# Attention with a mixture of adapters: value products on halves of the array, in two runs for each pair of heads

## The chip, the cores and the metric

The kernel runs on one core of one Trainium2 chip. The metric is the device time of one execution in microseconds. Before the change three runs gave a median of 231.32 us (231.14 to 232.71). Lower is better.

## What is computed

The reference has two parts. The first is attention with a relative position bias for 8 batches of 8 heads, 576 positions and 64 values a head:

```python
scores = q @ k.T / 8 + bias[bucket(|i - j|)]      # one bias table per head, 32 buckets
attn   = exp(scores - max) / sum(exp(scores - max))
x      = attn @ v                                 # heads side by side: 4608 rows of 512
```

All distances of 128 and more share one bucket, so the bias differs from a constant only in a band around the diagonal. The second part works on each row of x:

```python
logits = x @ w_gate                    # 8 experts; the best two are kept
w      = softmax over those two
out    = x + sum_e w[e] * (x @ A[e]) @ B[e]       # A: 512 x 16, B: 16 x 512
```

## The kernel before

**Units.** A unit is one batch and one pair of heads (a pair of heads fills the 128 partitions with its 2 x 64 values); there are 32 units in order, four to a batch. Scores are made transposed: keys on partitions, queries along the free axis. The keys of a head are four chunks of 128 (j = 0 to 3) and a tail of 64; the tails of a pair's two heads share one tile of 128 partitions (pe), while the chunks are in pm, laid out head, chunk, query.

**Slots.** The 4 x 576 = 2304 columns of a pair's chunks are cut into slots of 512, so a unit has six slots: s = 0 to 3 with 512 columns a head, s = 4 with the last 256, s = 5 for the tails. In each slot TensorE (PE) makes the scores of two heads on rows 0 to 63 and 64 to 127 of the array (lines 256 and 266) into one of two PSUM buffers, and ScalarE (ACT) takes the exponential of the slot in one instruction (lines 260 and 268). The scores of a slot therefore wait for the exponential of two slots earlier.

**The order is written by hand.** The loop at the end of the kernel names, for each slot, what every engine gets next; each engine works through its own list in that order. p is the unit before u; its products with the values are made during u. In a unit from the second batch on:

- slot 0: scores; on VectorE (DVE) the bias of chunk 3 of p; on PE the value products of chunk 0 of p, then the eight transposes of the next unit's keys and queries (line 224);
- slot 1: scores; an adapter step; DVE: bias of p's tail (line 274); value products of chunk 1; DVE copies the transposed keys and queries out (line 228);
- slot 2: scores, value products of chunk 2; slot 3: scores, an adapter step, value products of chunk 3, DVE: bias of chunk 0 of u;
- slot 4: scores, value products of p's tail; once a batch the transposes of the next batch's tails and their copy;
- slot 5: scores, an adapter step; DVE: finish p (reciprocal, line 313, and the normalising product, line 314), then bias of chunks 1 and 2 of u (line 285).

The bias is a product of the exponentials with a table of exponentials.

**Value products.** `values(u, j)` makes ten matmuls: five tiles of 128 queries for each head. For a chunk both operands have 128 keys on 128 partitions; for the tail, 64 keys, and the two heads lie on the two halves of the array. All of a pair accumulate in one PSUM tile of two banks (pv, a pool with one buffer), one bank a head, with 65 columns a query tile: 64 values and a column of ones that gives the sum. The first value product of a pair thus waits for line 314 of the pair before.

**Adapter steps.** When a batch is finished, its rows are put in groups of three tiles of 128, and each group becomes a queue of steps, each with a part for PE and one for DVE: transposes of x (line 342), logits and A (line 355, copied out by ACT, then the gates on DVE and GpSimd), transposes of the weighted z (line 394), and one product with B a tile (line 403), added to x on DVE (line 407) and stored. `place(slot)` emits the DVE part of the step before and puts the PE part of the next one into the given slot, after that slot's scores; `place(None)` emits the PE part at once. PE parts use a PSUM pool with two buffers (mm), which the transposes of keys, queries and tails use too.

**Last pairs.** In the first and the last unit of the last batch `early` packs the value products of p into slots 1 to 3 and finishes p in slot 3. After the loop, the products of the last pair alternate with the transposes of the last five tiles (class Last); these go through the mm pool, the third lot through the pool of the scores.

**Loads.** SyncE (SP) issues the loads of a batch head by head, two batches ahead; GpSimd (POOL) casts them to bf16, one pair at a time.

Of the kernel before, what the change touches and what calls it, by code (L numbers as in the profile page):

```python
# [11 lines left out]
FP32 = mybir.dt.float32  # L12
# [21 lines left out]
def kernel(  # L34
# [11 lines left out]
    nc = tc.nc  # L46
    B, H, S, D = q.shape
# [5 lines left out]
    HP = H // 2  # L53
# [6 lines left out]
    W = D + 1  # L60
# [81 lines left out]
    pool_cast = nc.gpsimd.tensor_copy  # L142
# [69 lines left out]
    xs, xe, probs, accs = {}, {}, {}, {}  # L212
    tps = {}

    def batch_tiles(b):
        if b not in qkT:
            qkT[b] = ldp.tile([128, HP, 2, S], BF16, name="qkT", tag="qkT")
        return qkT[b]

    def transpose_pe(u):  # L220
        ps = tps[u] = mp.tile([128, 2, 4, 128], BF16, name="tp", tag="mm")
        for i in range(2):
            for j in range(4):
# [46 lines left out]
    def bias(u, j, n=1):  # L270
        b, hp = units[u]
        pm, pe = probs[u]
        if j == 4:
            nc.vector.tensor_tensor(pe[:, S - TE:], pe[:, S - TE:],
                                    _ap(ebe, hp * TE + TE - 1, [[-1, TE]]), op=ALU.mult)
            return
        q0, q1 = max(0, (j - 1) * 128), min(S, (j + 2) * 128)
        e0 = 2 * hp * TW + TW - 1 - (q0 - (j - 1) * 128)
        w = q1 - q0
        if n == 1:  # L280
            t, e = pm[:, :, j * S + q0:j * S + q1], _ap(eb, e0, [[TW, 2], [-1, w]])
        else:
            t = _ap(pm, j * S + q0, [[4 * S, 2], [S + 128, n], [1, w]])
            e = _ap(eb, e0, [[TW, 2], [0, n], [-1, w]])
        nc.vector.tensor_tensor(t, t, e, op=ALU.mult)  # L285

    def values(u, j):
        b, hp = units[u]
        pm, pe = probs[u]
        vm, ve = vals[b % 2]  # L290
        if j == 0:
            accs[u] = pvp.tile([128, 2, 512], FP32, name="pv", tag="pv")
        pv = accs[u]
        for t in range(5):
            tok = min(t * 128, S - 128)
            for h in range(2):
                if j < 4:
                    lhsT = pm[:, h, j * S + tok:j * S + tok + 128]
                    rhs = vm[:, j, 2 * hp + h, :W]
                else:  # L300
                    keys = slice(h * 64, (h + 1) * 64)
                    lhsT, rhs = pe[keys, tok:tok + 128], ve[keys, hp, :W]
                nc.tensor.matmul(pv[:, h, t * W:(t + 1) * W], lhsT=lhsT, rhs=rhs,  # L303
                                 start=(j == 0 and t == 0), stop=(j == 4),
                                 skip_group_check=True)

    def normalise(u):
        b, hp = units[u]
        pv = accs.pop(u)
        if hp == 0:  # L310
            xs[b] = xp.tile([128, 5, Dm], BF16, name="xn", tag="xn")
        rc = ms.tile([128, 2, 5], FP32, name="rc", tag="rc")
        nc.vector.reciprocal(rc, _ap(pv, D, [[512, 2], [W, 5]]))  # L313
        nc.vector.tensor_tensor(  # L314
            _ap(xs[b], hp * 128, [[D, 2], [Dm, 5], [1, D]]),
            _ap(pv, 0, [[512, 2], [W, 5], [1, D]]),
            _ap(rc, 0, [[5, 2], [1, 5], [0, D]]), op=ALU.mult)
# [131 lines left out]
    def at(slot, fn, *args):  # L449
        due.setdefault(slot, []).append((fn, args))  # L450

    def place(pe_slot):
        if state["now"]:
            state["now"]()
            state["now"] = None
        if queue:
            pe, dve = queue.popleft()
            state["now"] = dve or (lambda: None)
            if pe is None:
                pass  # L460
            elif pe_slot is None:
                pe()
            else:
                at(pe_slot, pe)
# [114 lines left out]
    NU = len(units)  # L579

    def finish(p, t):
        normalise(p)
        if units[p][1] == HP - 1:
            at(t + 1, batch_done, units[p][0])

    for t in range(SLOTS * NU):
        u, s = divmod(t, SLOTS)
        b, hp = units[u]
        p = u - 1
        scores(u, s)  # L590
        for fn, args in due.pop(t, []):
            fn(*args)
        if u == 3:
            load_adapters(s)
        for i in range(3 if u < 2 else 2 if s % 3 == 0 else 1):
            if loading:
                loading.popleft()()
        early = u >= NU - HP and hp in (0, HP - 1)
        if s == 0:
            if u == 0:  # L600
                while loading:
                    loading.popleft()()
                loading = load(1)
            if p >= 0:
                bias(p, 3)
                if not early:
                    values(p, 0)
            if HP <= u < NU - 1:
                transpose_pe(u + 1)
            place(t + 1)  # L610
        if s == 1:
            if p >= 0:
                bias(p, 4)
                values(p, 1)
            if u + 1 < NU:
                if u >= HP:
                    transpose_out(u + 1)
                cast_v(u + 1, pool_cast)
        if s == 2:
            if p >= 0:  # L620
                values(p, 2)
                if early:
                    values(p, 3)
            if u + 2 < NU:
                cast_qk(u + 2, 0, pool_cast)
            place(t + 1)
        if s == 3:
            if p >= 0:
                values(p, 4 if early else 3)
            bias(u, 0)  # L630
            if early:
                finish(p, t)
        if s == 4:
            if p >= 0 and not early:
                values(p, 4)
# [12 lines left out]
        if s == 5:  # L648
            if u < HP:
                transpose_out(u + 1)  # L650
            if p >= 0 and not early:
                finish(p, t)
            if hp == 2 and b + 1 < B:
                cast_tails(b + 1, pool_cast)
            bias(u, 1, 2)
            if u in (NU - HP - 1, NU - 2, NU - 1):
                values(u, 0)
            if b >= B - 2:
                place(t + 1)


    u = NU - 1
    bias(u, 3)
    while state["now"] or queue:
# [2 lines left out]
                fn(*args)  # L667
        place(0)
    last = Last(B - 1)
    join(B - 1, 0, 384)  # L670
    values(u, 1)
    last.head_pe(0, 2, mp, "mm")
    bias(u, 4)
    values(u, 2)
    last.head_pe(2, 2, mp, "mm")
    values(u, 3)
    last.head_pe(4, 1, scp, "sc")
    values(u, 4)
    normalise(u)
    join(B - 1, 384, Dm)  # L680
    last.zl_pe(0, 3)
# [31 lines left out]
```

## Time and profile before

| | us |
|---|---|
| median of three runs | 231.32 |
| the profiled execution, its own time | 233.92 |
| its span, first to last instruction | 231.8 |
| exponentials, lines 260 and 268, ACT busy | 142.2 + 20.8 |
| value products of the chunks, line 303, PE busy | 63.0 |
| value products of the tails, line 303, PE busy | 10.2 |
| bias products of the chunks, line 285, DVE busy | 67.6 |
| normalising product, line 314, DVE busy | 26.4 |

The profile page gives, for each engine, the time in which it worked and the share of the span; then a chain, followed back from the last instruction, at each step to what released it. The waits say, for each instruction that an engine stood idle before, who ended that: total us, times, longest. A row of the timeline has a start, a duration, the engine, the line, the operation, out<-in, the shape (for a matmul first rows*columns of the array) and the count, and in brackets how long the engine had been idle and what ended that. PE overlaps matmuls, so the time from one start to the next says more of its pace than a duration. A row of the windows has a stretch, its length, busy us (and instructions) of PE, PE's weight loads, DVE, ACT and POOL, then the share of its clock that PE was granted, the DMA share and GB/s.

### The profile page before, as it was taken

How to read it: one execution, taken by the hardware profiler on the slowest of the kernel's cores; microseconds unless marked ns; L12 is line 12 of the kernel's file. 1: busy time of each engine (PE TensorE's matmuls, PEld its weight loads, DVE VectorE, ACT ScalarE, POOL GpSimd, SP SyncE). 2: the span in 40 equal slices, each digit the busy share in tenths (PEclk: the TensorE clock that was granted, in tenths of full speed). 3: DMA queues.
4: the chain of work that ended last, by engine and by line, in shares of the span. 5: the costliest groups of instructions: out<-in, count | busy, mean ns of one | idle time of the engine just before them, and what ended most of it. 6: DMA issues, size and time to landing. Idle time of an engine off the chain costs nothing.

```text
span 231.8 us, 7224 instructions
## 1 busy us (share of the span) xinstructions
PE 181.6 (78%) x2900; PEld 121.7 (52%) x2900; DVE 174.9 (75%) x401; ACT 174.0 (75%) x225; POOL 97.1 (42%) x171
## 2 busy tenths in 40 slices
PE   0797857989899976888899976897888887796661
PEld 0354534666566663564566664565565655464530
DVE  5346763878798869787998869987988788987760
ACT  3587954999899876879789876897988767877422
POOL 2316497249413613805903613916507443411010
PEclk9999985999999999899999999999999999999955
DMA  7899899878879998797597785976597122222206
GB/s 163 199 244 221 188 161 208 186 165 202 196 170 234 223 247 203 208 246 184 137 229 185 210 201 146 251 172 173 114 230 214 48 77 73 90 48 95 90 29 199
DMA packets 126521, 39.74 MB, mean 171 GB/s; under 512 B 120464, under 2 KB 121880, under 8 KB 126488
## 3 DMA queue, kind: packets, MB, share of 16 engines
q1 hardware_dynamic: 120056, 38.62, 68.2%
q0 software_dynamic: 4832, 0.27, 3.5%
q10 hardware_dynamic: 1600, 0.40, 0.8%
q8 instruction: 22, 0.36, 0.6%
q14 instruction: 11, 0.09, 0.1%
HBM read 29.84 MB, written 9.45 MB: 169 GB/s over the span
## 4 chain that ended last, share of the span: by engine, by line
DVE 36%; PE 34%; ACT 8%; SPq 8%; issue 6%; DMA 4%; POOL 2%; POOLq 0%; ACTq 0%
DVE pm L285 12%; PE pv L303 11%; PE sc L256 9%; DVE xn L314 7%; ACT pm L260 7%; DVE ot L407 6%; SPq L101 5%; PE dl L403 2%; PE xT_ps L342 2%; DVE xT L347 2%; DVE rc L313 2%; PE tp L224 2%; PE zl L355 2%; DMA q<-in_q_dram 2%; DVE qkT L237 1%
## 5 line engine op out<-in xcount | busy, mean ns | idle before, releaser
L260 ACT ACTIVATE pm<-sc 128x1024 bf16<-128x1024 f32 (+1 forms) x160 | 142.2, 939 | 31.2 <-PE sc L256 30.2
L303 PE MATMUL pv<-vm,pm 128*128 128x65 bf16 x1280 | 63.0, 197 | 9.2 <-DVE xn L314 9.1
L285 DVE TENSOR_TENSOR pm<-pm,eb 128x512 bf16<-128x512 bf16 (+2 forms) x96 | 67.6, 725 | 2.4 <-DMA eb<-gx_d 1.9
L303 PEld LDWEIGHTS <-pm 128*128 128x128 bf16 x1280 | 51.2, 99 | 33.8 <-issue 20.7
L256 PE MATMUL sc<-qkT 64*128 64x384 bf16 (+7 forms) x512 | 61.9, 300 | 4.7 <-ACT pm L260 1.8
L370 POOL TENSOR_TENSOR ls<-z,top 128x24 f32<-128x24 f32 (+1 forms) x11 | 4.1, 372 | 66.1 <-DVE top L368 57.5
L256 PEld LDWEIGHTS <-qkT 64*128 64x128 bf16 x512 | 19.2, 95 | 20.8 <-issue 6.6
L224 PE MATMUL tp<-ident,qkn 128*128 128x128 bf16 x256 | 21.1, 227 | 10.5 <-DVE qkn L129 5.6
L228 DVE COPY qkT<-tp 128x1024 bf16<-128x1024 bf16 x32 | 21.9, 683 | 8.9 <-PE tp L224 8.9
L314 DVE TENSOR_TENSOR xn<-pv,rc 128x640 bf16<-128x640 f32 x32 | 26.4, 824 | 1.1
L133 POOL CAST vm<-v 128x512 bf16<-128x512 f32 x32 | 22.1, 690 | 10.3 <-DMA v<-in_v_dram 10.3
L129 POOL CAST qkn<-q 128x512 bf16<-128x512 f32 x30 | 23.1, 771 | 3.0 <-DMA q<-in_q_dram 1.5
L129 POOL CAST qkn<-k 128x512 bf16<-128x512 f32 x32 | 20.9, 652 | 6.6 <-DMA k<-in_k_dram 6.5
L268 ACT ACTIVATE pe<-sc 128x576 bf16<-128x576 f32 x32 | 20.8, 650 | 3.2 <-PE sc L266 2.2
L224 PEld LDWEIGHTS <-qkn 128*128 128x128 bf16 x256 | 15.9, 101 | 11.8 <-DVE qkn L129 5.6
L407 DVE TENSOR_TENSOR ot<-dl,xn 128x512 f32<-128x512 f32 x28 | 19.1, 683 | 2.8 <-PE dl L403 2.8
L266 PE MATMUL sc<-qkT 64*64 64x64 bf16 (+1 forms) x128 | 14.1, 294 | 7.5 <-ACT pm L260 7.3
L403 PE MATMUL dl<-Bc,zT 128*128 128x512 bf16 x31 | 12.2, 393 | 4.3 <-DVE ot L407 3.7
L313 DVE RECIPROCAL rc<-pv 128x10 f32<-128x10 f32 x32 | 6.9, 215 | 10.2 <-PE pv L303 10.2
L347 DVE COPY xT<-xT_ps 128x1024 bf16<-128x1024 bf16 (+1 forms) x20 | 11.2, 562 | 1.2 <-PE xT_ps L342 1.2
L266 PEld LDWEIGHTS <-qkT 64*64 64x64 bf16 x128 | 6.7, 105 | 9.3 <-issue 6.8
L385 POOL TENSOR_TENSOR gate<-nu,rd 128x24 f32<-128x24 f32 (+1 forms) x11 | 2.6, 239 | 19.4 <-DVE rd L383 8.7
(87 smaller groups left out, 164.8 us busy)
## 6 DMA issues: line engine op xcount, KB each, us to landing
q<-in_q_dram SPq DMA_DIRECT2D x64, 128.0 KB, 3.1
v<-in_v_dram SPq DMA_DIRECT2D x64, 128.0 KB, 2.9
k<-in_k_dram SPq DMA_DIRECT2D x62, 128.0 KB, 2.9
out_dram<-ot SPq DMA_DIRECT2D x28, 256.0 KB, 2.2
qke<-in_q_dram SPq DMA_DIRECT2D x8, 128.0 KB, 2.8
ve<-in_v_dram SPq DMA_DIRECT2D x16, 64.0 KB, 2.6
out_dram<-otL SPq DMA_DIRECT2D x4, 256.0 KB, 2.0
qke<-in_k_dram SPq DMA_DIRECT2D x7, 128.0 KB, 2.8
```

Of the source, the lines that this page charges most:

```text
L129: eng(out=nats[u][:, i].rearrange("p j (h d) -> p j h d", h=2), in_=src)
L133: eng(out=vals[b % 2][0][:, :, 2 * hp:2 * hp + 2, :D], in_=staged[b][2][:, :, 2 * hp:2 * hp + 2, :])
L224: nc.tensor.transpose(ps[:, i, j, :], nats[u][:, i, j, :], ident)
L228: nc.vector.tensor_copy(batch_tiles(b)[:, hp, :, :512], tps.pop(u).rearrange("p i j t -> p i (j t)"))
L256: nc.tensor.matmul(sc[:, h, c - SW * s:c - SW * s + w], lhsT=kT[rows, j * 128:(j + 1) * 128], rhs=qT[rows, q0:q0 + w], start=True, stop=True)
L260: nc.scalar.activation(pm[:, :, SW * s:end], sc[:, :, :n], ACT.Exp, scale=scale)
L266: nc.tensor.matmul(flat[rows, q0:q0 + n], lhsT=kT[rows, 512:], rhs=qT[rows, q0:q0 + n], start=True, stop=True)
L268: nc.scalar.activation(pe, flat[:, :S], ACT.Exp, scale=scale)
L285: nc.vector.tensor_tensor(t, t, e, op=ALU.mult)
L303: nc.tensor.matmul(pv[:, h, t * W:(t + 1) * W], lhsT=lhsT, rhs=rhs, start=(j == 0 and t == 0), stop=(j == 4), skip_group_check=True)
L314: nc.vector.tensor_tensor(_ap(xs[b], hp * 128, [[D, 2], [Dm, 5], [1, D]]), _ap(pv, 0, [[512, 2], [W, 5], [1, D]]), _ap(rc, 0, [[5, 2], [1, ...
L407: nc.vector.tensor_tensor(ot, self.dl, self.x[t], op=ALU.add)
```

## The change

`values` takes a run, cross = 0 or 1, and the chunks to be made. Each product has 64 keys: the two halves of the array work on different heads at once. In run 0 the lower half takes head 0 and the upper half head 1, in run 1 the other way round, so that in both the halves write to different banks. The tails, which lie on halves already, belong to run 0. A pair has 50 products in run 0 and 40 in run 1.

Run 0 of p is made as a block in slot 1, run 1 in slot 4. The bias of p's tail moves to slot 0, behind that of chunk 3. The transposes of the next unit move from slot 0 to slot 2, the copy of their result from slot 1 to slot 3 (in the first four units they stay in slots 4 and 5). Of the three adapter steps of a unit the one of slot 1 is now emitted in slot 0, right behind the scores; in the last two batches the fourth step, which stood in slot 0, follows run 0 in slot 1. The `early` cases go. After the loop the last pair's run 0 is finished first, then come the transposes of the last tiles, all in the mm pool, then run 1.

```diff
-    def values(u, j):
+    def values(u, cross, *js):
         b, hp = units[u]
         pm, pe = probs[u]
         vm, ve = vals[b % 2]
...
+        for j in js:
+            if j == 0 and not cross:
+                accs[u] = pvp.tile([128, 2, 512], FP32, name="pv", tag="pv")
+            pv = accs[u]
+            for t in range(5):
+                tok = min(t * 128, S - 128)
+                for half in range(2):
+                    h = half ^ cross
+                    keys = slice(half * 64, (half + 1) * 64)
+                    if j < 4:
+                        lhsT = pm[keys, h, j * S + tok:j * S + tok + 128]
+                        rhs = vm[keys, j, 2 * hp + h, :W]
+                    else:
+                        lhsT, rhs = pe[keys, tok:tok + 128], ve[keys, hp, :W]
+                    nc.tensor.matmul(pv[:, h, t * W:(t + 1) * W], lhsT=lhsT, rhs=rhs,
+                                     start=(j == 0 and t == 0 and not cross),
+                                     stop=(j == 3 and cross == 1),
+                                     skip_group_check=True)
...
         if s == 0:
...
             if p >= 0:
                 bias(p, 3)
-                if not early:
-                    values(p, 0)
+                bias(p, 4)
+            place(None)
+        if s == 1:
+            if p >= 0:
+                values(p, 0, 0, 1, 2, 3, 4)
+            if u + 1 < NU:
+                cast_v(u + 1, pool_cast)
+            if b >= B - 2:
+                place(None)
+        if s == 2:
             if HP <= u < NU - 1:
                 transpose_pe(u + 1)
-            place(t + 1)
...
             place(t + 1)
         if s == 3:
+            if HP <= u < NU - 1:
+                transpose_out(u + 1)
+            bias(u, 0)
+        if s == 4:
             if p >= 0:
-                values(p, 4 if early else 3)
...
+                values(p, 1, 0, 1, 2, 3)
...
         if s == 5:
...
-            if p >= 0 and not early:
+            if p >= 0:
                 finish(p, t)
...
-            if u in (NU - HP - 1, NU - 2, NU - 1):
-                values(u, 0)
-            if b >= B - 2:
-                place(t + 1)
+            if u == NU - 1:
+                values(u, 0, 0, 1, 2)
...
     last = Last(B - 1)
+    bias(u, 4)
+    values(u, 0, 3, 4)
+    last.head_pe(0, 2, mp, "mm")
     join(B - 1, 0, 384)
-    values(u, 1)
-    last.head_pe(0, 2, mp, "mm")
-    bias(u, 4)
-    values(u, 2)
     last.head_pe(2, 2, mp, "mm")
-    values(u, 3)
-    last.head_pe(4, 1, scp, "sc")
-    values(u, 4)
+    last.head_pe(4, 1, mp, "mm")
+    values(u, 1, 0, 1, 2, 3)
     normalise(u)
```

More of the change, by code (lines that the diff above doesn't have):

```diff
@@ L290, in values @@
         vm, ve = vals[b % 2]
[L291 to L305, printed above, removed]
+        for j in js:
[16 more added lines that the diff above has]
+                                     skip_group_check=True)
     def normalise(u):
@@ L597 @@
                 loading.popleft()()
-        early = u >= NU - HP and hp in (0, HP - 1)
         if s == 0:
@@ L605 @@
                 bias(p, 3)
-                if not early:
-                    values(p, 0)
+                bias(p, 4)
[8 more added lines that the diff above has]
+        if s == 2:
             if HP <= u < NU - 1:
                 transpose_pe(u + 1)
-            place(t + 1)
[L611 to L623, printed above, removed]
             if u + 2 < NU:
@@ L627 @@
         if s == 3:
+            if HP <= u < NU - 1:
+                transpose_out(u + 1)
+            bias(u, 0)
+        if s == 4:
             if p >= 0:
-                values(p, 4 if early else 3)
[L630 to L633, printed above, removed]
-            if p >= 0 and not early:
-                values(p, 4)
+                values(p, 1, 0, 1, 2, 3)
             if u + 2 < NU:
@@ L650 @@
                 transpose_out(u + 1)
-            if p >= 0 and not early:
+            if p >= 0:
                 finish(p, t)
```

## The prediction

> **What bounds the kernel now.** I read the page's busy shares and chain first.
>
> ```profile
> PE 181.6 (78%) x2900; PEld 121.7 (52%) x2900; DVE 174.9 (75%) x401; ACT 174.0 (75%) x225; POOL 97.1 (42%) x171
> DVE 36%; PE 34%; ACT 8%; SPq 8%; issue 6%; DMA 4%; POOL 2%; POOLq 0%; ACTq 0%
> ```
>
> Three engines are busy for three quarters of the span, none for all of it, and the chain hops between DVE and PE. So the pace is set by a loop between these two. The waits name its links:
>
> ```profile
> ACT pm L260 <- PE sc L256: 30.2, 49, 4.2
> DVE rc L313 <- PE pv L303: 10.2, 14, 2.2
> PE pv L303 <- DVE xn L314: 9.1, 14, 1.2
> ```
>
> ACT starves for scores (30.2 us). DVE's reciprocal waits for the last value product (only 14 of 32 times: otherwise DVE itself is late), and the next pair's first value product waits for DVE to empty the one accumulator. I call the start of a pair's reciprocal R. The timeline's reciprocals stand at 114.52 (unit 16) and 165.14 (unit 24): 6.33 us from R to R. ACT's exponentials alone need 5.0.
>
> What a value product costs shows in the timeline of PE:
>
> ```profile
> 105.75 0.48 PE L303 MATMUL pv<-vm,pm 128*128 128x65 bf16 x10
> 106.16 0.39 PE L256 MATMUL sc<-qkT 64*128 64x192 bf16 x4
> 106.48 0.39 PE L403 MATMUL dl<-Bc,zT 128*128 128x512 bf16 x1
> 106.71 0.47 PE L303 MATMUL pv<-vm,pm 128*128 128x65 bf16 x10
> 107.12 0.28 PE L256 MATMUL sc<-qkT 64*128 64x256 bf16 x2
> 107.24 0.31 PE L303 MATMUL pv<-ve,pe 64*128 64x65 bf16 x10
> 107.48 0.40 PE L234 MATMUL tpe<-ident,qke 128*128 128x128 bf16 x4
> ```
>
> Read starts. 256 score columns followed by 64-row products take 0.12 us (107.12 to 107.24), 512 followed by a 128-row product 0.32 (106.16 to 106.48), not 0.24: leaving one row mode for the other costs 0.08 to 0.1. Ten 128-row products and such an exit take 0.41, so 0.031 each. Ten 64-row ones and an exit take 0.24 (107.24 to 107.48): 0.14 for five couples, 0.028 a couple.
>
> **The change, part by part.**
>
> *PE's work.* Before, a pair has 40 products on 128 rows and 10 on 64; after, 90 on 64 rows, 45 couples. 32 pairs: 1280 x 0.031 + 160 x 0.028 = 44.2 us against 1440 x 0.03 = 43.2 (I take 0.03). Mode changes, counted in the two instruction orders, fall from 314 to 222: 92 x 0.1 = 9.2 us. So PE gives up 10 us in all, 0.32 a pair.
>
> A rule speaks against this. The Trainium skill, "TensorE: Matmul & The Clock Gate", section "LDWEIGHTS (loading the stationary operand)", says that a weight load's time goes by its columns, so half the rows cost as much; an estimate from its figure (128 columns at 1.2 a ns, 107 ns a load) makes the 1280 loads more 137 us if they stood in a row. In the trace ten 64-row loads take 0.30 us, ten 128-row ones 0.36, so two halves load together. I go by the rows.
>
> *The loop.* Before, each chunk of keys has its own slot, and the late bias products are needed late: chunk 3's by slot 3, the tail's by slot 4. After, the first run holds chunks 0 to 3 and the tail in one block in slot 1; its last four products need the tail's bias, and the scores of slot 2 stand behind them on PE. DVE's order up to there:
>
> ```profile
> 152.47 0.22 DVE L313 RECIPROCAL rc<-pv 128x10 f32<-128x10 f32 x1 [0.26 <-PE pv L303]
> 152.73 0.82 DVE L314 TENSOR_TENSOR xn<-pv,rc 128x640 bf16<-128x640 f32 x1
> 153.47 1.35 DVE L285 TENSOR_TENSOR pm<-pm,eb 128x1536 bf16<-128x1536 bf16 x2
> ...
> 160.74 2.04 DVE L285 TENSOR_TENSOR pm<-pm,eb 128x1536 bf16<-128x1536 bf16 x2
> ...
> 163.29 0.62 DVE L274 TENSOR_TENSOR pe<-pe,ebe 128x192 bf16<-128x192 bf16 x1
> ```
>
> With the groups' means, 0.215 + 0.824 + 1.027 + 0.628 + 0.323 = 3.02, less 0.15 by which starts overlap ends: R + 2.87. Before, PE went on at R + 1.07. Two couples more, and slot 2's scores start at R + 2.97.
>
> Hand schedule of a unit without adapter steps, **after**: scores at 2.97, exponential 0.43 later (167.13 to 167.56 is such a step) for 1.02, slot 4's scores at 4.47 (their buffer waits for it), second run at 4.59, 20 x 0.03 and 0.2 of latency: next R at **5.4**. **Before**: v0 1.12, 0.33 and 0.54 with the transposes, scores 2.0, two exponentials 2.43, 3.34 to 4.36, slot 4's scores 4.40, ten tail products 4.52, next R **4.87**; measured 5.37 in unit 24. PE's 0.32 is gone, the bias wait has taken its place.
>
> With adapter steps DVE decides. Unit 21, after: 2.87, an output add 0.62 twice, key/query copy 0.62, bias 0.42, transposed-input copy or add 0.62, a little for the gates: 5.95; before, the same instructions and PE's step after the first of them: 5.95 (measured 6.44). Where a pair has the tails' transposes in slot 4 (units 19, 23), DVE's tail copy waits for them in both; after, PE gets there 0.6 sooner: 6.95 against 7.55 (7.30 measured). Unit 18 loses: its logits are moved from slot 1, behind the scores, to slot 0, ahead of them. Their last third needs the copy that DVE makes after the tail's bias, R + 3.25; scores 1, the whole first run 0.76 and scores 2 queue behind it: 7.1 against 6.2.
>
> | unit | 17 | 18 | 19 | 20 | 21 | 22 | 23 | 24 | sum |
> |---|---|---|---|---|---|---|---|---|---|
> | measured before | 5.40 | 6.02 | 7.31 | 6.52 | 6.44 | 6.26 | 7.30 | 5.37 | 50.6 |
> | by hand, before | 5.3 | 6.2 | 7.55 | 6.0 | 5.95 | 5.9 | 7.55 | 4.85 | 49.3 |
> | by hand, after | 5.4 | 7.1 | 7.0 | 6.2 | 5.95 | 5.5 | 6.95 | 5.4 | 49.5 |
>
> The middle is a draw: +0.4 for units 9 to 24. Units 5 to 8 (few steps; 21.6 measured) come to 22.3: +0.7. In units 25 to 31 a fourth step moves from slot 5 to slot 1, behind the first run and ahead of scores 2: +0.5.
>
> *Start.* Units 2 and 3 lose 1.0 to 1.3 each (bias wait, and a second run of 0.6 where ten products of 0.3 stood ahead of the transposes), but unit 4's transposes waited 0.84 and 1.58 us for POOL's casts; they move from slot 0 to slot 2 and that wait is absorbed, with the 4.2 us hole of ACT behind it: -1.0 net. SP issues its loads in the same order, POOL its casts too up to unit 25.
>
> *End.* Before, the last pair's products alternate with the transposes of the last tiles and only ten tail products follow the last bias; R(31) to the last reciprocal takes 5.07. After: DVE has 2.5 to bias 3, 0.3, two adds 1.8 with their waits, bias 4 at R + 4.9. Behind its last four products PE holds 15 transposes; the third lot now uses the two-buffer pool and waits for ACT's 0.80 copy of the first; then the whole second run 0.6: 4.95 + 0.43 + 0.2 + 0.80 + 0.3 + 0.6 + 0.25 = 7.5. +2.4.
>
> Sum: -1.0 + 0.7 + 0.4 + 0.5 + 2.4 = **+3.0 us**. The profiled execution took 233.9 (span 231.8), so it would be 236.9; it lies 2.6 above the median of the runs shown, 231.3, and one half-clock stretch (91.6 to 95.0) explains 1.4 of that. On the median: **234.3**.
>
> **Rivals.**
>
> 1. *PE's saving comes through* (not slower). For it: ACT's 30.2 us wait is for PE, and before's hand schedules run 1.3 us short of the measured eight units, so PE's queueing costs more than I see. Against it: DVE's 18 late reciprocals. If two thirds of 10 us arrive and the end still loses 2.4, with the start's 1.0: 231.3 - 6.7 + 1.4 = 226; if the end is hidden too, 222. It decides where the tail's bias ends before R + 2.3.
> 2. *The bias wait is longer* (slower by much). Rows above: 2.04 for the two bias products and 0.62 for the tail's where POOL casts run beside them, instead of 1.35 and 0.25. Before, this was hidden until slots 3 and 4; after, it lies on the loop: +0.7 to 1.0 in, say, 10 units. With it comes the clock:
>
> ```profile
> 88.20:91.60 3.40, 1.51 (x25) 1.11 (x26) 3.40 (x6) 2.47 (x3) 2.07 (x3) 1.00 0.93 210
> 91.60:95.00 3.40, 3.40 (x40) 2.05 (x38) 2.04 (x6) 1.98 (x2) 1.83 (x4) 0.50 0.74 172
> 139.40:142.80 3.40, 2.09 (x29) 1.24 (x26) 3.33 (x9) 2.68 (x5) 2.31 (x4) 1.00 0.41 91
> ```
>
>    A stretch with PE (first figure) busy for 1.51 of 3.40 us is followed by one at half clock (0.50, third figure from the end); after 2.09 it is not. Unit 18's wait would fall under it, and its twin in unit 10. Each stretch costs about 1.4 (unit 13 took 7.82, its twin 21 6.44). 234.3 + 8 + 2 x 1.4 = 245.
> 3. *Couples don't hold their rate in long runs* (the change doesn't do what it says). The trace has only five in a row, at 0.028; without deducting the exit, 0.048. At 0.05 the second run lies 0.4 a unit longer on the loop: 31 x 0.4 = 12, so 247; one by one at 0.03 each, +19, 253.
> 4. *A draw*: the end's loss met by a gain of the DVE-late units, 231.
>
> **How the numbers follow.** A change under 1% (229.0 to 233.6) can hardly be told from none here. Forecast, 232 to 237: 0.40, most of it over 233.6. Rival 1: 0.24. Rival 2: 0.17. Rival 3: 0.05. Rival 4: 0.14. Faster 0.24, same 0.22 (rival 4 and 0.08 of the forecast), slower 0.54. The range reaches from the middle of rival 1 to that of rival 2 with a tenth left out on each side, 226 to 243; the slower cases' own range is 233.6 to 245.
>
> **What would show it.** Right: PE's busy time down by some 10 us, the wait of PE's value products for the tail's bias (pe) in nearly every unit, ACT's waits moved from slot 1 to slot 2, R to R between 5.4 and 7.1, and over 7 us from R(31) to the last reciprocal. Wrong: R to R near 5.0 to 5.5 in the units with steps (rival 1), half-clock stretches by the handful (rival 2), a second run of over 0.8 us (rival 3), or the last transposes finding the second run done.

## The result, and the profile after

The changed kernel takes **244.89 us** (median of four, 241.31 to 245.97), the kernel before, run beside it, 231.9: a ratio of 1.047 (95% interval 1.034 to 1.060), 13.0 us slower. (Ratios, here and below, leave out executions well above the fastest of the same kernel, so that they need not equal the quotient of the medians.) The forecast was 234.3: the sign was right, the size was 10.6 us short, and the result lies at the very edge of the range given for the slower cases (233.6 to 245). The profiled execution took 245.47 us with a span of 243.3 (233.92 and 231.8 before), so the two spans differ by 11.5.

The page's busy shares and chain, which stand beside those shown of before:

```profile
PE 189.8 (78%) x4180; PEld 125.5 (52%) x4180; DVE 177.4 (73%) x401; ACT 172.6 (71%) x225; POOL 96.6 (40%) x171
DVE 44%; PE 32%; ACT 9%; issue 6%; DMA 3%; SPq 3%; POOL 1%; POOLq 0%; DVEq 0%
```

DVE's share of the chain rose from 36% to 44%: more of the path runs through DVE, although DVE has the same 401 instructions. The waits (engine and line, what it waits for, us in total, times, the longest) say what stands behind it:

```profile
ACT pm L260 <- PE sc L256: 32.4, 32, 2.5
DVE qkT L228 <- PE tp L224: 25.3, 24, 4.9
PE pv L311 <- DVE pm L285: 13.5, 27, 0.9
DVE rc L322 <- PE pv L311: 6.9, 11, 2.4
PE pv L311 <- DVE xn L323: 2.7, 5, 0.9
PE pv L311 <- DVE pe L274: 2.3, 7, 1.0
```

The third line is new: in 27 waits the value products stand still for the bias products on the chunks. The wait for the accumulator, the fifth line, fell from 9.1 us to 2.7. The tail's bias, the last line, adds little idle time of its own, since PE has mostly waited already when it is wanted. One pair shows how it looks, in the timeline of unit 12 (rows of PE and DVE, and one of ACT; start, length, engine, operation, and in brackets the idle time ahead of it with what ended it); the reciprocal that opens it is R:

```profile
87.17 0.21 DVE L322 RECIPROCAL rc<-pv 128x10 f32<-128x10 f32 x1
87.31 0.38 PE L351 MATMUL xT_ps<-ident,xe 128*128 128x128 bf16 x4
87.42 0.83 DVE L323 TENSOR_TENSOR xn<-pv,rc 128x640 bf16<-128x640 f32 x1
87.62 0.39 PE L256 MATMUL sc<-qkT 64*128 64x64 bf16 x4
88.16 1.69 DVE L285 TENSOR_TENSOR pm<-pm,eb 128x1536 bf16<-128x1536 bf16 x2
88.30 0.33 PE L311 MATMUL pv<-vm,pm 64*128 64x65 bf16 x10 [0.28 <-DVE xn L323]
89.51 0.67 PE L311 MATMUL pv<-vm,pm 64*128 64x65 bf16 x30 [0.89 <-DVE pm L285]
89.78 0.25 DVE L274 TENSOR_TENSOR pe<-pe,ebe 128x192 bf16<-128x192 bf16 x1
...
90.01 0.31 PE L311 MATMUL pv<-ve,pe 64*128 64x65 bf16 x10
90.16 0.38 PE L256 MATMUL sc<-qkT 64*128 64x128 bf16 x4
...
90.58 1.94 ACT L260 ACTIVATE pm<-sc 128x1024 bf16<-128x1024 f32 x2 [1.24 <-PE sc L256]
```

Chunk 0's ten products start at 88.30 and PE then stands still for 0.89 us: chunks 1 to 3 wait for DVE's bias products, which DVE starts only behind the reciprocal and the normalising product. Slot 2's scores (64x128, at 90.16) start at R + 2.99, and ACT's gap of 1.24 follows at once.

The table puts reciprocals of all profiles used here side by side (us from the start of the span, read from the timeline). R(u) is the reciprocal made in unit u, and unit u runs from R(u-1) to R(u). The last two columns are the time of half granted clock ahead of R(31), and the seven intervals R(8) to R(15), all at full clock (in the first and the fourth row R(16) to R(23), the same kinds of pairs, since a half-clock stretch falls into the other seven).

| kernel | R(4) | R(8) | R(16) | R(24) | R(31) | last | span | half clock | seven pairs |
|---|---|---|---|---|---|---|---|---|---|
| before | 40.8 | 62.4 | 114.5 | 165.1 | 211.7 | 216.7 | 231.8 | 10.2 | 45.25 |
| after | 44.7 | 68.1 | 121.2 | 175.7 | 221.4 | 228.6 | 243.3 | 34.0 | 45.86 |
| before, nobody waits for a bias | 42.3 | 64.1 | 115.4 | 168.3 | 214.9 | 219.9 | 235.0 | 10.2 | 46.01 |
| after, nobody waits for a bias | 38.8 | 60.2 | 115.2 | 168.0 | 215.3 | 222.6 | 237.2 | 6.8 | 47.46 |
| after, chunk 1's bias early | 41.7 | 64.3 | 116.8 | 168.9 | 215.6 | 224.1 | 238.8 | 20.4 | 45.51 |
| before, the moves alone | 38.7 | 60.4 | 110.2 | 161.3 | 208.5 | 213.6 | 228.1 | 13.6 | 44.41 |

At full clock seven pairs cost only 0.6 us more than before. What is far larger is the time at half clock: 34.0 us against 10.2. A pair that falls under such a stretch costs more than its twin eight pairs earlier: unit 20 takes 7.55 us, unit 12 6.22; units 16 and 24, each under a double stretch, 7.22, unit 8 5.30.

### The profile page after: what moved, and what is told of

Its sections match the earlier page's. It is cut to its first block, busy times and chain, and to the rows that moved or that the text cites. A ratio compares the mean times of both kernels' runs of the same rounds, so it can differ in the third digit from the quotient of the medians.

```text
span 243.3 us, 9784 instructions
## 1 busy us (share of the span) xinstructions
PE 189.8 (78%) x4180; PEld 125.5 (52%) x4180; DVE 177.4 (73%) x401; ACT 172.6 (71%) x225; POOL 96.6 (40%) x171
## 4 chain that ended last, share of the span: by engine, by line
DVE 44%; PE 32%; ACT 9%; issue 6%; DMA 3%; SPq 3%; POOL 1%; POOLq 0%; DVEq 0%
DVE pm L285 17%; PE pv L311 11%; DVE xn L323 10%; PE sc L256 8%; ACT pm L260 7%; PE tp L224 5%; DVE ot L416 4%; DVE pe L274 3%; DVE rc L322 2%; DVE qkT L228 2%; PE xT_ps L351 2%; DMA k<-in_k_dram 2%; DVE xT L356 2%; SPq L101 1%; DVE qkT L237 1%
## 5 line engine op out<-in xcount | busy, mean ns | idle before, releaser
L311 PE MATMUL pv<-vm,pm 64*128 64x65 bf16 x2560 | 61.2, 197 | 17.1 <-DVE pm L285 13.5
L311 PEld LDWEIGHTS <-pm 64*128 64x128 bf16 x2560 | 54.5, 98 | 27.6 <-DVE pm L285 18.4
L256 PEld LDWEIGHTS <-qkT 64*128 64x128 bf16 x512 | 21.4, 98 | 36.1 <-issue 23.8
L379 POOL TENSOR_TENSOR ls<-z,top 128x24 f32<-128x24 f32 (+1 forms) x11 | 2.5, 231 | 76.0 <-DVE top L377 65.7
L224 PE MATMUL tp<-ident,qkn 128*128 128x128 bf16 x256 | 23.3, 243 | 7.6 <-DVE qkn L129 5.6
L129 POOL CAST qkn<-k 128x512 bf16<-128x512 f32 x32 | 23.3, 728 | 7.3 <-DMA k<-in_k_dram 7.3
L224 PEld LDWEIGHTS <-qkn 128*128 128x128 bf16 x256 | 17.5, 108 | 14.6 <-DVE qkn L129 5.6
L311 PE MATMUL pv<-ve,pe 64*128 64x65 bf16 x320 | 12.7, 200 | 2.5 <-DVE pe L274 2.3
L412 PE MATMUL dl<-Bc,zT 128*128 128x512 bf16 x31 | 11.8, 388 | 1.1 <-DVE ot L416 0.7
L364 PE MATMUL zl<-AW,xT 128*128 128x136 bf16 x124 | 10.0, 230 | 2.5 <-DVE xT L356 2.5
L274 DVE TENSOR_TENSOR pe<-pe,ebe 128x192 bf16<-128x192 bf16 x32 | 11.7, 365 | 0.0
```

Source lines behind the costliest of these rows:

```text
L129: eng(out=nats[u][:, i].rearrange("p j (h d) -> p j h d", h=2), in_=src)
L256: nc.tensor.matmul(sc[:, h, c - SW * s:c - SW * s + w], lhsT=kT[rows, j * 128:(j + 1) * 128], rhs=qT[rows, q0:q0 + w], start=True, stop=True)
L274: nc.vector.tensor_tensor(pe[:, S - TE:], pe[:, S - TE:], _ap(ebe, hp * TE + TE - 1, [[-1, TE]]), op=ALU.mult)
```

## The experiments

Two theories stood at the start. **The bias wait**: the first run needs every bias at once, early in the pair; the wait itself and the half clock that comes with it make the loss. **The places**: what costs is what was moved around the runs, and the half-row products have little to do with it. All ratios are to the kernel before, with 95% intervals.

### Places against half rows

Full-row products in the changed kernel's places: chunks 0, 3 and the tail in slot 1, chunks 1 and 2 in slot 4.

```diff
-                        lhsT = pm[keys, h, j * S + tok:j * S + tok + 128]
-                        rhs = vm[keys, j, 2 * hp + h, :W]
+                        lhsT = pm[:, h, j * S + tok:j * S + tok + 128]
+                        rhs = vm[:, j, 2 * hp + h, :W]
...
-                values(p, 0, 0, 1, 2, 3, 4)
+                values(p, 0, 0, 3, 4)
...
-                values(p, 1, 0, 1, 2, 3)
+                values(p, 1, 1, 2)
```

> The changed order with products on all 128 rows again: chunks 0, 3 and the tail in slot 1, chunks 1 and 2 in slot 4; nothing is left out. If the places are to blame (slot 2's scores stand behind a block that waits for the tail's bias), it is as slow as the changed kernel or slower, since PE has its 100 mode changes back: 242 to 250 us. If the half-row products themselves cost the time, it goes back to 230 to 236.

Measured: 250.49 us (246.93 to 251.69), ratio 1.077 (1.071 to 1.083). In the same places the half-row products are 5.6 us faster than full-row ones, and seven pairs at full clock take 45.86 in the change against 46.80 here. The two forms differ a little in more than the rows: slot 1's block holds chunks 0 and 3 and the tail here, all chunks in the change. So the halves do seem to save time on PE; the order around them loses 17.5, more than three times as much.

### The clock: idle products as a filler

24 idle couples stand between chunk 2 and chunk 3 of the first run, to keep PE busy in the wait. They go to columns 384 and up of the accumulator, of which only 325 a bank are read, so the result stays the same.

```diff
+            if j == 3 and not cross and u < NU - 1:
+                for t in range(FILL):          # 24
+                    for half in range(2): nc.tensor.matmul(accs[u][:, half, 384:384 + W], ...)
```

> The changed kernel with 24 couples of idle products (0.72 us at 0.03) into unused columns of the accumulator, between chunk 2 and chunk 3 of the first run, where PE waits for a bias in nearly every unit; the output does not use them. If the half-clock stretches make the loss, most of those in the middle go and the time falls to 235 to 239. If the wait itself makes it, the time stays at 242 to 246, with or without such stretches; if PE is the bound, it rises by up to 20.

Measured: 253.22 us (250.41 to 256.05), ratio 1.076 (1.070 to 1.081). The profile has less half clock ahead of R(31), 20.5 us (13.7, 3.4 and 3.4), and is slower all the same: seven pairs at full clock take 48.12 instead of 45.86, 0.32 us more for each pair. The filler, itself 0.72 us long by estimate, was only partly in the wait. Two of its executions had a mean granted clock of 0.96, above the best of the change (0.943), and took 250.4 and 251.0 us. It says that paying on the path for a better clock is no bargain; it doesn't settle what the clock costs.

### Is it the tail's bias?

The crossed run, chunks 0 to 3, goes first; the straight run with the tail goes to slot 4. Only the tail's bias is taken out of the wait.

```diff
-                values(p, 0, 0, 1, 2, 3, 4)
+                values(p, 1, 0, 1, 2, 3)
...
-                values(p, 1, 0, 1, 2, 3)
+                values(p, 0, 0, 1, 2, 3, 4)
```

> The changed kernel with the two runs swapped: the crossed run, which has no tail, in slot 1, the straight run with the tail in slot 4 (the last pair keeps its order). The tail's bias is then wanted three slots later; chunk 3's is still wanted in slot 1. If the bias wait is the cause, a unit's loop is 0.3 to 0.5 us shorter and fewer stretches fall to half clock: 229 to 237. If it is something else, 242 to 246.

Measured: 244.34 us (242.62 to 246.54), ratio 1.046 (1.039 to 1.054): no difference to the change. Yet the tail's bias is the last link of the change's block, as the prediction has it. Its unit 22:

```profile
157.25 0.66 DVE L274 TENSOR_TENSOR pe<-pe,ebe 128x192 bf16<-128x192 bf16 x1
...
157.97 0.24 PE L311 MATMUL pv<-ve,pe 64*128 64x65 bf16 x4 [0.23 <-DVE pe L274]
...
158.04 0.38 PE L256 MATMUL sc<-qkT 64*128 64x128 bf16 x4
```

The last four products start when the tail's bias ends, and slot 2's scores follow at once. So it is in 18 of the units 5 to 24: these scores start 0.13 to 0.32 us after the end of the tail's bias (in units 10 and 18 an adapter step holds the block up for longer). With the runs swapped they start at R + 3.10 on average instead of R + 3.34 (units 5 to 31), and seven pairs at full clock still take 46.08 (45.86 in the change). What the run shows is that these 0.24 us a unit buy nothing; that the second run is five couples longer may eat some 0.15 of them (an estimate, 5 x 0.03).

### The runs spread over the slots

The crossed run is cut: chunks 0 to 2 in slot 0, chunk 3 in slot 1, the straight run with the tail in slot 4; transposes and adapter steps go back to their old places. In the second form only chunk 0 stays in slot 0 and chunks 1 to 3 go to slot 1.

```diff
         if s == 0:
+                values(p, 1, 0, 1, 2)        # second form: values(p, 1, 0)
+            if HP <= u < NU - 1:
+                transpose_pe(u + 1)
+            place(t + 1)
...
-                values(p, 0, 0, 1, 2, 3, 4)
+                values(p, 1, 3)              # second form: values(p, 1, 1, 2, 3)
...
-                values(p, 1, 0, 1, 2, 3)
+                values(p, 0, 0, 1, 2, 3, 4)
```

> Half-row products in the places of the kernel before: crossed run of chunks 0 to 2 in slot 0 and of chunk 3 in slot 1, straight run with the tail in slot 4; transposes, copies, adapter steps and biases where they were before the change; at the end the last transposes stand ahead of the last straight run. If the places made the loss and the saving on PE is real, it is faster than before: 222 to 230. If half-row products cost more than they save, 234 or more. If PE's time is worth nothing, 230 to 233.

> The run before it (half-row products in the old places) with chunks 1 and 2 of the crossed run moved from slot 0 to slot 1, behind slot 1's scores and the adapter step; only chunk 0, whose bias is long done, is left in slot 0 ahead of the transposes. If the 271 us came from biases that were wanted in slot 0, it falls to 233 to 245; if from half-row products in general, it stays over 255.

Measured: 271.25 us (269.04 to 272.11), ratio 1.163 (1.156 to 1.169), and in the second form 249.53 (249.32 to 251.55), ratio 1.075 (1.071 to 1.080). The timeline of the first form shows why it is the slowest of all:

```profile
126.99 0.33 PE L312 MATMUL pv<-vm,pm 64*128 64x65 bf16 x10 [1.16 <-DVE xn L324]
128.13 0.73 PE L312 MATMUL pv<-vm,pm 64*128 64x65 bf16 x20 [0.82 <-DVE pm L285]
```

The biases of chunks 1 and 2 are now wanted in slot 0, ahead of the scores of slot 1: PE stands still first for the accumulator and then for the bias. Two chunks whose biases are wanted one slot earlier cost 22 us. The second form has no half clock from 37.4 to 228.5 us of its span and still loses 17 us (seven pairs at full clock take 48.33), with 25 couples in slot 4; both forms also carry the transposes in slot 0, which turn out below to cost much in such an order.

### Nobody waits for a bias

The bias products write to a tile of their own, in the changed kernel and in the kernel before. The bias is thereby left out of the result; DVE does the same instructions in the same order, and no value product waits for them.

```diff
-            nc.vector.tensor_tensor(pe[:, S - TE:], pe[:, S - TE:],
+            nc.vector.tensor_tensor(aside[:, :TE], pe[:, S - TE:],
...
-        nc.vector.tensor_tensor(t, t, e, op=ALU.mult)
+        nc.vector.tensor_tensor(o, t, e, op=ALU.mult)      # o lies in the tile aside
```

> The changed kernel with the bias products written to a tile that nothing reads, so the bias is left out of the result; DVE does the same work in the same order, but no value product waits for it. If the wait of the block for DVE's biases makes the loss, it goes to 222 to 230 us. If half-clock stretches, PE's order or the half-row products make it, it stays at 240 to 246.

> The kernel before, with its bias products written aside in the same way (the bias is left out of the result). Its value products want each chunk's bias late, so little should change: 228 to 232 us. If it gains as much as the changed kernel does from this, the bias wait is no part of the difference.

Measured: the change 239.14 us (237.26 to 240.2), ratio 1.028 (1.022 to 1.034); the kernel before 235.48 (233.41 to 236.76), ratio 1.012 (1.006 to 1.018). Writing aside costs the kernel before some 3 us, so the two are compared with each other: **the 13.0 us between them shrink to 3.7**. Some 9 us of the loss hang on the waits for biases. The half clock goes with them: 6.8 us ahead of R(31) instead of 34.0. In the table R(31) differs by 0.4 and the span by 2.2, but the pairs are no draw: without the waits the change is 3.5 ahead at R(4), loses 3.9 from there to R(31) and 2.3 more to the last reciprocal. The price of writing aside blurs this. At full clock seven pairs take 46.01 with it in the kernel before (45.25 without) and 47.46 in the change (45.86 without), although nobody waits; and DVE stands idle 6.5 us in all ahead of the bias products of chunk 3 and the tail in the change, 3.7 in the kernel before, nothing where they are written in place. So some of the 3.7 may be the experiment's own price, and the 9 is an estimate.

There is no gain, though PE is busy for less: 176.8 us against 181.4. One place where that went shows in the changed form's timeline, in slot 2:

```profile
145.49 0.61 PE L225 MATMUL tp<-ident,qkn 128*128 128x128 bf16 x8 [1.55 <-DVE ot L421]
```

The moved transposes wait for a PSUM buffer that DVE frees with its adapter work. Over the whole profile transposes wait 16.4 us for a buffer that DVE frees with its copies and adds, against 5.8 in the kernel before where nobody waits and 0.7 in the change. With the bias out of the way this is the next link from DVE to PE.

### One bias early

The bias of chunk 1 goes to slot 4, ahead of the pair's reciprocal; everything else stays as in the change.

```diff
+            bias(u, 1)           # slot 4
...
-            bias(u, 1, 2)        # slot 5
+            bias(u, 2)
```

> The changed kernel with the bias of chunk 1 made in slot 4, ahead of the reciprocal, instead of together with chunk 2's behind it: some 0.5 us less between the reciprocal and the first run's biases. If that chain of DVE is the loop, 0.3 to 0.5 us a unit: 229 to 236 us. If not, 242 to 246; if DVE's reciprocal is made late by it, over 246.

Measured: 239.93 us (237.9 to 241.91), ratio 1.029 (1.024 to 1.034). One bias product, split off and put earlier in DVE's order, gives back 5.0 of the 13.0 us, and the result is complete. All biases behind the reciprocal end earlier by it, the tail's too: slot 2's scores start at R + 2.90 on average instead of R + 3.34 (units 5 to 31). At full clock seven pairs gain only 0.35 (45.51 against 45.86); half clock ahead of R(31) falls from 34.0 to 20.4, and R(4) comes 3.0 earlier.

### The moves

Some 4 us were left to explain, and the moves were the suspect. The first run makes only the moves, in the kernel before; the second undoes them in the change; the third undoes them and has chunk 1's bias early.

```diff
 # before, the moves alone (undone in the other two)
         if s == 0:
-            if HP <= u < NU - 1:
-                transpose_pe(u + 1)
-            place(t + 1)
+            place(None)
         if s == 1:
-                if u >= HP:
-                    transpose_out(u + 1)
+            if b >= B - 2:
+                place(None)
         if s == 2:
+            if HP <= u < NU - 1:
+                transpose_pe(u + 1)
         if s == 3:
+            if HP <= u < NU - 1:
+                transpose_out(u + 1)
         if s == 5:
-            if b >= B - 2:
-                place(t + 1)
```

> The kernel before with the moved parts alone: the transposes from slot 0 to slot 2, their copy from slot 1 to slot 3, the adapter steps of slots 0 and 5 issued at once in slot 0 and slot 1; value products, bias products and the end stay as before. Theory A (the moves are the rest that the bias wait leaves, about 4 us): 235 to 238, with PE's transposes waiting in slot 2 for DVE's adapter parts. Theory B (the moves cost nothing, the rest is the end's 2.1 us and the clock): 231 to 233.5.

> The changed kernel with the transposes back in slot 0, their copy in slot 1 and the adapter steps where they were before; both runs of value products and the end as in the change. Theory A (the moves cost 3 to 4 us, and the transposes ahead of the first run fill PE's wait for the bias): 238 to 241. Theory B (they cost nothing): 243 to 246, since the first run's wait for the bias of chunk 1 is as long as before and PE stands still behind it anyway.

> As the run before (transposes and adapter steps back in their old places), and the bias product of chunk 1 in slot 4, ahead of the pair's reciprocal. If the two causes add (5 us from the bias of chunk 1, 3 to 4 from the moves): 233 to 237, of which 2 are the end. If the moves cost nothing: 239 to 241. Below 231 only if half-row products also bring PE's 10 us in, once nobody waits.

Measured: the moves alone **230.28 us** (229.09 to 231.63, ten runs), ratio 0.9905 (0.9865 to 0.9944); the change without them 258.9 (255.5 to 305.65), ratio 1.105 (1.092 to 1.119); the change without them and with chunk 1's bias early 244.62 (243.55 to 246.94), ratio 1.054 (1.044 to 1.064). Both theories were wrong: the moves cost nothing, they are a gain, of 2.3 us in the kernel before, 4.7 with chunk 1's bias early (244.62 against 239.93), and 14.0 in the change (258.9 against 244.89). The profile of the second is of an execution of 305.65 us, far above its other three (255.5 to 259.58; see the end), so the mechanism is read from the third. Selected rows of its unit 12, the pair shown of the change above:

```profile
83.89 0.21 DVE L322 RECIPROCAL rc<-pv 128x10 f32<-128x10 f32 x1
84.03 0.61 PE L224 MATMUL tp<-ident,qkn 128*128 128x128 bf16 x8
...
84.56 0.39 PE L256 MATMUL sc<-qkT 64*128 64x64 bf16 x4
...
85.91 0.35 DVE L408 COPY zT<-zT_ps 128x384 bf16<-128x384 bf16 x1
...
86.31 0.38 PE L351 MATMUL xT_ps<-ident,xe 128*128 128x128 bf16 x4 [1.36 <-DVE zT L408]
86.63 0.78 PE L311 MATMUL pv<-vm,pm 64*128 64x65 bf16 x40
...
87.39 0.60 PE L256 MATMUL sc<-qkT 64*128 64x128 bf16 x8
```

Transposes and adapter steps share a pool of two PSUM buffers. With the keys' transposes in slot 0 one buffer is taken, the other holds zT, and the adapter's next transposes wait 1.36 us on PE until DVE has copied zT, behind reciprocal, normalising and bias. The whole first run and slot 2's scores queue behind: these start at R + 3.50, in the change at R + 2.99, and that although the first run no longer waits for a bias. The same pair of the kernel before with the moves:

```profile
79.24 0.21 DVE L313 RECIPROCAL rc<-pv 128x10 f32<-128x10 f32 x1
...
80.36 0.47 PE L303 MATMUL pv<-vm,pm 128*128 128x65 bf16 x10 [0.93 <-DVE xn L314]
80.67 0.38 PE L342 MATMUL xT_ps<-ident,xe 128*128 128x128 bf16 x4
...
81.55 0.48 PE L303 MATMUL pv<-vm,pm 128*128 128x65 bf16 x10 [0.17 <-DVE pm L285]
...
81.96 0.39 PE L256 MATMUL sc<-qkT 64*128 64x128 bf16 x4
```

The adapter's transposes find a free buffer, chunk 1's products wait 0.17 for their bias, and slot 2's scores start at R + 2.72; without the moves they start at R + 3.29 in this pair. Over the whole profile the waits of transposes for a buffer fall with the moves from 5.4 us to 2.0 in the kernel before, and from 6.5 to 3.2 with chunk 1's bias early. That agrees with gains of 2.3 and 4.7, but no run separates it from the mere place of the keys' transposes, which stand ahead of slot 1's scores without the moves and behind slot 2's with them. This kernel, 1% faster than the kernel before, is the best of the study.

### Only the middle in halves

With chunk 1's bias early, the first four and the last two pairs go back to full-row products in the old slots, with the old end.

```diff
+        if 0 <= p < 4 and s < 5:
+            whole(p, s)              # chunk s, or the tail, on 128 rows as before
...
-    values(u, 0, 3, 4)
-    last.head_pe(0, 2, mp, "mm")
+    whole(u, 1)
+    last.head_pe(0, 2, mp, "mm")
```

> The change with the bias product of chunk 1 in slot 4, and the first four and the last two pairs of heads on 128-row products in the places of the kernel before, the end too; the two runs of half-row products remain for pairs 4 to 29. Measured so far: 239.9 us for the same with all pairs in halves, 230.3 for the kernel before with the moves alone; in their profiles the former is 3.0 us later at the fifth reciprocal, 3.7 more at the last but one, and 3.4 more from there to the last. Theory A (the half-row runs are a draw in the middle once chunk 1's bias is early; what is left sits in the start and the end): 232 to 235. Theory B (the runs cost in every pair, start and end are only where it shows first): 236 to 239.

Measured: 239.97 us (238.99 to 241.09), ratio 1.036 (1.024 to 1.047): no gain over 239.93. Theory A falls as put; the time is a little above theory B's range too. In the profile R(4) comes 1.7 earlier (39.94 against 41.68), but seven pairs at full clock take 45.94, and the end isn't mended: R(31), which is in slot 3 as before, to the last reciprocal takes 8.75 where the kernel before has 5.07. One line says what is late:

```profile
218.14 0.39 PE L423 MATMUL zT_ps<-ident,zt 128*128 128x128 bf16 x2 [2.96 <-POOL zt L416]
```

PE waits 2.96 us for the last adapter group's gates. In the kernel before pair 27, which closes batch 6, is finished in slot 3 instead of slot 5, and its adapter steps enter the queue two slots earlier; the change dropped that exception with the early branch, and this run did not restore it. That this is the cause of the whole end was not tried.

## Why the prediction was right in sign and short in size

**The terms of the sum**, from the two profiles:

| term | forecast | measured |
|---|---|---|
| start, to R(4) | -1.0 | +3.9 |
| units 5 to 8 | +0.7 | +1.8 |
| units 9 to 24 | +0.4 | +4.8 |
| units 25 to 31 | +0.5 | -0.8 |
| end, R(31) to the last reciprocal | +2.4 | +2.1 |

The measured ones come to 11.8, and 0.3 is gained back after the last reciprocal: 11.5, the difference of the spans.

**What held.** Couples keep their rate in long runs: in unit 12 the second run's forty products start at 92.29 and slot 5's scores at 92.98, 0.69 us for twenty couples at 0.03 and an exit of 0.09; rival 3 is out. Slot 2's scores were put at R + 2.97, right behind the products that need the tail's bias, and stand at R + 2.99 there, released in that way (R + 3.30 in unit 21; in units 9 to 15 from R + 2.65 to R + 4.22). A unit without adapter steps was put at 5.4 and takes 5.30 at full clock (unit 8). The hand schedule's verdict on the middle, a draw, nearly holds at full clock: +0.6 in seven pairs, so about 1.4 in sixteen. ACT's gaps for scores moved from slot 1 (12.6 us in units 5 to 31) to slot 2 (21.8). The end was put at 7.5 from R(31) to the last reciprocal and took 7.19, with its links: four products that wait for the tail's bias until R + 4.55, and a third lot of transposes that waits 0.55 us for ACT's copy.

**What failed: the clock was left out of the forecast.** Units 9 to 24 came out 3.4 over those 1.4, and there the change has some 15.6 us of half clock (115.7 to 122.6, 143.0 to 146.5, and 170.3 to 177.2, of which 1.5 lie behind R(24)) against 3.4. Units 16 and 24, which fall under two of these, take 7.22 each against 5.37 before. The prediction had priced such a stretch at 1.4 and put all of it into rival 2, which said 245. That rival came to the right size by a partly wrong way: it priced the longer bias products in ten pairs at 8 us and two stretches at 2.8. That is luck in part. The waits at full clock cost little; the stretches are seven more before R(31), not two. What they cost together is only estimated. At the 1.3 of units 20 and 12 the seven come to 9 us. Whole executions say less: those of the change run from a span of 239.2 us at a mean clock of 0.943 to 243.8 at 0.905, which is 4.6 us for some 19 more at half clock (twice the missing share of the clock times the span), so 0.24 each, and 6 us for the 23.8 more. No run changed the clock alone.

**What failed: the start.** The -1.0 rested on unit 4's transposes, and there the gain came: unit 4 takes 6.58 us instead of 9.29. But R(1) comes 1.2 later, and units 2 and 3 lose 2.7 each where 1.0 to 1.3 had been put: the start has stretches at half clock from 20.2 to 30.4, 33.8 to 37.2 and 40.6 to 44.1 (before: 33.6 to 40.4), and R(4) comes 3.9 later. Where nobody waits for a bias R(4) is at 38.8 in the change and 42.3 in the kernel before: the gain is there, and the bias wait, with the half clock that goes with it, turns it round.

**What was left out of the link.** The prediction named the tail's bias, the last in DVE's order, put its end at R + 2.87 and priced only this end. The end came as put in unit 12 (R + 2.86), but 0.24 us less of it, with the runs swapped, moved nothing; moving chunk 1's bias, which shortens all of the wait by about 0.4, gave 5.0 us back. What has no place in the sum is that a block of five chunks stops at its first unready operand, with PE idle from then on (13.5 us for the chunks' biases, 2.3 for the tail's), and what idle time does to the clock.

**What failed: the moved steps.** They were costed at nothing in most units and as a loss in unit 18 (7.1 against 6.02; it takes 6.75). Alone they gain 2.3 us, and the change would be 14.0 slower without them. The prediction followed each step's place on DVE and PE but not the two PSUM buffers. Against the kernel before with the moves alone, all the rest of the change (the two runs, the `early` cases, the end) costs 14.6 us.

**PE's saving.** The sign named for it, PE's busy time down by 10 us, did not appear: 189.8 against 181.6, at a mean clock of 0.920 against 0.955. In the two kernels in which nobody waits it is down by 4.6, and in equal places the halves gain 5.6. So about half of the 10 us seems real, and none of it reached the end: with slot 2's scores at R + 1.87 in unit 12, where nobody waits, that unit still takes 6.40 us (6.22 in the change), held up by a transpose that waits 1.27 for a buffer. Rival 1 fails on this.

**Open.** With chunk 1's bias early the change still loses 9.7 us to the kernel before with the moves. At R(4) their profiles differ by 3.0, from there to R(31) by 4.1 and from R(31) to the last reciprocal by 3.4. Putting the old order back at the start and, but for pair 27, at the end did not move the median; it made the start 1.7 shorter and the end no shorter. How much of the rest is clock, and what the early finish of pair 27 is worth, was not separated.

## What to carry to other kernels

A block that gathers the products of several chunks needs all their operands at once: before gathering, list when each operand becomes ready, and move the producer of the first late one ahead, here a bias product ahead of the reciprocal. Follow the PSUM buffers of a moved step as well as its engines: the moves of transposes and adapter steps, costed at nothing, went with fewer waits for a buffer and gained, while the change they were made for lost. Where the profile before already shows stretches at half clock, waits of PE of half a microsecond each are to be priced with the half clock that may follow them, in the forecast itself.

## What was unexpected of the hardware

**The clock's condition isn't PE's busy share of one stretch alone.** Windows of 3.4 us of the changed kernel's profile (first figure PE busy, third from the end the granted clock):

```profile
112.30:115.70 3.40, 2.09 (x30) 0.89 (x25) 2.88 (x7) 2.92 (x5) 1.41 (x3) 1.00 0.73 194
115.70:119.10 3.40, 2.80 (x52) 2.04 (x52) 2.47 (x4) 0.92 (x2) 3.40 (x5) 0.50 0.36 81
228.40:231.80 3.40, 2.04 (x35) 1.49 (x25) 2.36 (x6) 0.51 (x2) 0.00 (x0) 1.00 0.00 0
231.80:235.20 3.40, 0.76 (x6) 0.40 (x7) 2.41 (x13) 0.37 (x2) 0.93 (x1) 1.00 0.00 0
```

PE busy for 2.09 us was followed by half clock, and for 2.04 it was not; nor was it in two other windows with less, 1.92 us from 225.0 to 228.4 and 2.02 from 132.6 to 136.0 of the kernel before. The prediction's reading (1.51 is followed by half clock, 2.09 is not), taken from two windows, doesn't make a rule. The Trainium skill, "TensorE: Matmul & The Clock Gate", section "HAM oscillation — how this bites in real kernels", gives as its abstract rule that PE have no idle gaps over some 3.4 us. The longest in the first of these windows is 0.87 us, and the clock was halved all the same, so that rule alone doesn't cover this case.

**A granted clock of 1.00 in the records doesn't have to mean full pace.** In the profile of the execution of 305.65 us the records show 1.00 throughout, yet forty half-row products take 1.27 us to the next start (126.76 to 128.03). In the change they take 1.24 under half clock (119.86 to 121.10) and 0.69 at full clock (92.29 to 92.98). So PE went at the pace of half clock while the records say full; whether the clock was halved there and the records missed it, or something else slowed PE, no run shows.
